# Attention, routing and expert layers in one kernel: row sums of shared blocks added with the even head, and another order of the attention plan

## The chip, the cores and the metric

One core of a Trainium2 chip runs the whole kernel in one launch. The metric is the device time of one execution in microseconds (us); the median of several runs counts. The engines are TensorE (PE, matmuls; PEld is its weight loads), VectorE (DVE), ScalarE (ACT), GpSimd (POOL) and SyncE (SP, which here only issues DMAs). Each executes its own queue in order.

## The reference

Attention over 2 x 8 heads of 576 rows and 64 columns with rotary embedding; a layer of eight experts of which each of 1152 tokens takes two; a dense feed-forward layer with softplus.

```python
scores = scale * np.matmul(q_rot, k_rot.transpose(0, 1, 3, 2))
scores = scores - np.max(scores, axis=-1, keepdims=True)
attn = np.exp(scores)
attn = attn / (np.sum(attn, axis=-1, keepdims=True) + 1e-09)
attn_out = np.matmul(attn, v)
...
top2 = np.argpartition(-noisy_logits, 2, axis=1)[:, :2]
h = np.maximum(x[mask] @ w1[e], 0.0)
out[mask] += top2_w[mask, k, None] * (h @ w2[e])
...
h = x @ w_in
g = np.maximum(h, 0.0) + np.log1p(np.exp(-np.abs(h)))
return g @ w_out
```

## The kernel before

Attention comes first, then the experts in order of their load, then the feed-forward layer. The last two are written out in their order; matmuls there are done in three parts (high by high, high by low, low by high half of a split number). The change touches attention alone, which is not written in an order: each step is entered in a table `plan` with engine, estimated cost, a due place and its predecessors (`op`, L1054), and `schedule` (L58) makes a list schedule of it: of the steps that can start, the one that starts earliest goes next, and of equal ones that with the smaller due place. `AHEAD` (L39) shifts the due place of each kind of step. The schedule's order is the order in which the instructions are written, and so that of each engine's queue.

Heads are worked in eight pairs p; head g is 2p or 2p + 1. A pair has nine blocks n of 128 score rows: four of each head, and a fifth, whose 128 rows are the last 64 of both heads. The steps, by their names in the plan:

- `S` (PE, `emit_S`, L486): scores of block n into one of two PSUM buffers, 4 matmuls, 8 for a shared block. `M` (DVE, L499): negated row maximum. `E` (ACT, `emit_exp`, L508): exponent, with the row sums as a second output (`acc`).
- `T` (PE, L517; the four columns that are left, L521 and L523), `Th` (ACT, L549), `Tl` (DVE, L553): transposes of the exponents for one block, their high and low halves. Two PSUM buffers `pt`.
- `A` (PE, L564, L566): two halves a = 0, 1 of the product with the values, 9 matmuls each, `Ao` (ACT) takes it out. `X` (PE, L586): transposes it back together with the gating logits. `rs` (POOL, `row_sum`), `ri` (DVE, L598): 1 / (row sum + 1e-9). `Xl`, `Xd` (DVE, L602, L611): scale logits and rows. `Xd` frees the PSUM buffer and, after an odd head, sends the rows to memory.
- `prep` (PE, L413), `ph`, `pl` (ACT, DVE): transposes of a pair's rotated queries and keys and their halves; `dq` and `dk` (SP, L449, L453): copy the queries, then the keys, to the other half of the partitions. The first `S` of pair p waits for `dk`. In pair 0 ACT does this instead (`k2`). `ro` and `rope` (POOL), for pair 0 `rf` (DVE): the rotation. `vs` (POOL): split of the values.
- `R`, `RP`, `RF`: routing of the first 512 tokens, in 14 steps; `cr`, `ga` (POOL, `gather_A`): gather the first expert's rows, which `XT` (PE, L1041), `XTh` and `XTl` transpose and split. `sp` (ACT, L183) and `sl` (DVE, the first two on POOL, L187): round and split six weight chunks.

PSUM buffers `pa` (two) are shared by `A`, `X`, `prep`, `XT` and the routing matmuls, in the order of their issue. In `row_sum` (L589) two small adds are done for each head: one for its four blocks, from `sums`, and one for its 64 rows of the shared block, from `sumL`.

Of the kernel before, what the change touches and what calls it, by code (L numbers as in the profile page):

```python
# [10 lines left out]
F32 = mybir.dt.float32  # L11
# [6 lines left out]
OP = mybir.AluOpType  # L18
# [4 lines left out]
B, H, S, D = 2, 8, 576, 64  # L23
N, DM, E, F1 = B * S, H * D, 8, 1024
# [13 lines left out]

AHEAD = {'A0': 30288.5, 'A1': 3627.5, 'Ao0': 4788.8, 'Ao1': -14676.7, 'E': 18585.3, 'L': -1902, 'M': 16742.7,  # L39
# [7 lines left out]
FC = 384  # L47
# [57 lines left out]
def fused_kernel(ctx: ExitStack, tc: tile.TileContext, q, k, v, w_gate, w_noise, noise, w1, w2,  # L105
                 w_in, w_out, cs_t, out):
    nc = tc.nc
# [205 lines left out]
    at1 = at_ctx.enter_context(tc.tile_pool(name="at1", bufs=1))  # L313
# [19 lines left out]
    sums = at1.tile([128, B, 5, H], F32, name="sums")  # L333
# [4 lines left out]
    PL = at1.tile([128, S], F32, name="PL")  # L338
    sumL = at1.tile([128, H], F32, name="sumL")

# [161 lines left out]
    def emit_exp(n):  # L502
        p, h, i = block(n)
        ps, nmx = stS.pop(n)
        g = 2 * p + h
        b = g // H
        acc = sumL[:, p:p + 1] if i == 4 else sums[:, b, i + b, g % H:g % H + 1]
        nc.scalar.activation(P_of(n).rearrange("p (a c) -> p a c", a=2), ps[:, :, :HN], AF.Exp, bias=nmx, scale=1.0,  # L508
                             accum_out=acc)
# [79 lines left out]
    def row_sum(g):  # L589
        b, h = divmod(g, H)  # L590
        nc.gpsimd.tensor_scalar(rinv[:, b, b:b + 4, h], sums[:, b, b:b + 4, h], 1e-9, None, op0=OP.add)
        q, j = slice(64 * b, 64 * b + 64), 4 - 4 * b
        x = 64 * (g % 2)
        nc.gpsimd.tensor_scalar(rinv[q, b, j:j + 1, h], sumL[x:x + 64, g // 2:g // 2 + 1], 1e-9, None, op0=OP.add)

# [467 lines left out]
    for n in range(NSTEP):  # L1063
        p, h, i = block(n)
        g, at_ = 2 * p + h, 10 * p + 5 * h + i
        twice = [("dk", p)] if p else [
            ("k2", x, u) for x in range(2) for u in ((0, 1, 2) if i == 4 else (h, 2))]
        need = twice + [("pl", p, u) for u in ((0, 1, 2) if i == 4 else (h, 2))]
        if i == 4:
            reads = [("T", g - 2, 5), ("T", g - 2, 4)] * (p > 0)  # L1070
        else:
            two = 2 * g + i // 2 - 3
            reads = readers(two // 2, two % 2 * 2 + i % 2) if two >= 0 else []
        op(("S", n), "PE", 1056 if i == 4 else 528, at_ - 4, need + [("S", n - 1)] * (n >= 1) + [("E", n - 2)] * (n >= 2), emit_S, n)
        op(("M", n), "DVE", 674, at_ + 7, [("S", n)], emit_max, n)
        op(("E", n), "ACT", 717, at_ + 69, [("M", n)] + reads +
           ([("rf", 5)] if n in (2, 3) else prep0 if n in (5, 6) else []), emit_exp, n)
    for g in range(2 * NP_):
        p, h = divmod(g, 2)
        for u in range(6 - h):  # L1080
            n = 5 * g + (0, 1, 2, 3, 3, 4)[u]
            blk = [9 * p + 5 * h + i for i in range(4)]
            src = [9 * p + 4] if u == 5 else blk[u:u + 1] if u < 4 else blk + [9 * p + 4] * (h == 0)
            op(("T", g, u), "PE", 400 if u != 4 else 200 if h else 300, n, [("E", e) for e in src], emit_T, g, u)
            old = (g - 2, g - 1) if u == 5 or u == 4 and h == 0 else (g - 2,)
# [9 lines left out]
        n = 5 * g + 5  # L1095
        op(("rs", g), "POOL", 620, n - 8000, [("E", 9 * p + i) for i in (range(4, 9) if h else range(5))], row_sum, g)
        op(("ri", g), "DVE", 190, n - 60, [("rs", g)], row_inv, g)
        op(("X", g), "PE", 1110, n - 24, [("Ao", g, 0), ("Ao", g, 1), ("c", 0)], emit_X, g)
        op(("Xl", g), "DVE", 150, n - 67, [("X", g), ("ri", g)], X_lg, g)
        op(("Xd", g), "DVE", 400, n - 67, [("Xl", g)], X_x, g)  # L1100
    for p in range(NP_):
        n = 10 * p
# [25 lines left out]
        if p:  # L1128
            op(("dq", p), "SP", 2000, n, [("pl", p, u) for u in range(3)] + [("S", 9 * p - 10)] * (p > 1), move_queries, p)
            op(("dk", p), "SP", 2000, n, [("dq", p)], keys_twice, p)  # L1130
    op(("in", 0), "SP", 5400, -300, [], lambda: None)
    op(("in", 1), "SP", 1300, -299, [("in", 0)], lambda: None)
# [21 lines left out]
    op(("cr", 0), "POOL", 2300, 100, [("R", 8)], choose_rest)  # L1154
    op(("ga", 0), "POOL", 2200, 100, [last[0], ("S", 62), ("vs", 7), ("Xd", 9)], gather_A)
    op(("gl", 0), "SP", 500, 100, [("ga", 0)], lambda: None)
# [519 lines left out]
```

## Time and profile before

| | |
|---|---|
| median of 3 runs | 661.6 us (661.05 to 663.89) |
| the profiled execution, its time and its span | 662.88 us, 661.1 us |
| busy in the span: PE, PEld | 622.8 us (94%), 560.9 us (85%) |
| busy: DVE, ACT, POOL | 482.0 (73%), 424.6 (64%), 218.0 us (33%) |
| mean granted clock of TensorE | 0.986 |
| DMA | 109.79 MB, mean 166 GB/s |

All rows below are from one execution. Attention takes the time up to about 188 us; there PE, DVE and ACT are all busy for most of the time. The experts and the feed-forward layer follow and are nearly all PE. A row of an engine in order of time gives the start, the duration, the line of the program, the instruction with what it writes and reads, and in brackets the idle time of that engine before it and what seems to have ended it. PEclk is the clock that was granted to TensorE as a share of its full speed: 1.0 is 2.4 GHz and 0.5 is 1.2 GHz.

### The profile page before, as it was taken

To read this page: it belongs to the slowest core of one execution; us is meant where nothing else is said; L and a number is where in the kernel's file an instruction comes from. 1 tells how busy PE (TensorE), PEld (TensorE's weight loads), DVE (VectorE), ACT (ScalarE), POOL (GpSimd) and SP (SyncE) were. 2 spreads that over 40 slices of the span, in tenths; PEclk is the share of its full clock that TensorE was granted. 3 is DMA by queue.
4 is the path that set the end of the run, shared out by engine and by line. 5 is a ranking of instruction groups with operands and counts; after the bars stand their busy time and mean duration, and the time that the engine had idled before them with its cause. 6 is when DMAs were issued, how large, how long until landed. Compare 5 with 4: busy or idle time off the path is not lost.

```text
span 661.1 us, 11470 instructions
## 1 busy us (share of the span) xinstructions
PE 622.8 (94%) x3922; PEld 560.9 (85%) x3922; DVE 482.0 (73%) x997; ACT 424.6 (64%) x887; POOL 218.0 (33%) x302
## 2 busy tenths in 40 slices
PE   3799999998798999999999999989999999999997
PEld 2699999898696998988889798968789999899996
DVE  6689888987774767859686776846996665676664
ACT  4788888877742666757667575736866544565553
POOL 6876766728545203341424231412310100000000
PEclk9899999999979999999999999998999999999999
DMA  6645465861635949998899989775410100100000
GB/s 156 152 100 136 124 149 126 267 185 39 203 113 183 321 150 315 334 332 291 315 311 323 312 291 351 273 222 176 144 49 32 34 17 0 49 1 1 33 0 33
DMA packets 69629, 109.79 MB, mean 166 GB/s; under 512 B 11616, under 2 KB 39008, under 8 KB 69120
## 3 DMA queue, kind: packets, MB, share of 16 engines
q1 hardware_dynamic: 63280, 93.31, 45.7%
q0 software_dynamic: 3136, 10.10, 4.6%
q10 hardware_dynamic: 3152, 5.62, 2.3%
q8 instruction: 32, 0.52, 0.3%
q14 instruction: 29, 0.24, 0.1%
HBM read 76.70 MB, written 23.59 MB: 152 GB/s over the span
## 4 chain that ended last, share of the span: by engine, by line
PE 62%; issue 3%; DVE 1%; DMA 1%; ACT 1%; POOL 0%; DVEq 0%; POOLq 0%; ACTq 0%
PE p L263 9%; PE p L264 9%; PE p L265 9%; PE ph L263 5%; PE ph L264 5%; PE ph L265 5%; PE po L265 5%; PE po L264 5%; PE po L263 5%; PE p L1242 2%; PE pa L1198 1%; PE p L1244 1%; DMA yg<-ytab,yrow 1%; PE px L1491 0%; DVE wc L187 0%
## 5 line engine op out<-in xcount | busy, mean ns | idle before, releaser
L187 DVE TENSOR_TENSOR w<-wraw,w 128x1024 fp32r<-128x1024 f32 x73 | 99.4, 1373 | 0.7 <-ACT w L183 0.7
L183 ACT ACTIVATE w<-wraw 128x1024 fp32r<-128x1024 f32 x75 | 78.8, 1056 | 12.9 <-DMA wraw<-in_moe_w_dram 12.1
L232 POOL TENSOR_TENSOR dm<-dm,da 128x512 int32<-128x512 int32 x32 | 42.0, 1312 | 134.1 <-DVE da L229 69.1
L264 PE MATMUL p<-xl,w 128*128 128x320 f32 (+3 forms) x256 | 77.5, 303 | 0.3 <-DVE xl L1201 0.3
L263 PE MATMUL p<-xh,w 128*128 128x320 f32 (+3 forms) x256 | 77.4, 302 | 0.0
L265 PE MATMUL p<-xh,w 128*128 128x320 f32 (+3 forms) x256 | 77.3, 302 | 0.0
L1554 ACT ACTIVATE fa<-ph 128x256 f32<-128x256 f32 (+1 forms) x64 | 26.0, 407 | 69.4 <-PE ph L265 69.4
L499 DVE TENSOR_REDUCE nmx<-ps 128x1 f32<-128x576 f32 x72 | 54.2, 753 | 17.6 <-PE ps L486 17.5
L263 PE MATMUL ph<-xh,w 128*128 128x256 f32 (+1 forms) x192 | 58.5, 305 | 1.0 <-ACT xh L1496 0.7
L263 PE MATMUL p<-w,hb 128*128 128x512 f32 x144 | 58.7, 407 | 0.0
L264 PE MATMUL ph<-xl,w 128*128 128x256 f32 (+1 forms) x192 | 57.5, 300 | 0.3 <-DVE xl L1497 0.3
L265 PE MATMUL ph<-xh,w 128*128 128x256 f32 (+1 forms) x192 | 57.4, 299 | 0.0
L1218 DVE SCALAR_TENSOR_TENSOR hb<-p,hb 128x256 fp32r<-128x256 f32 (+1 forms) x104 | 31.8, 347 | 34.1 <-ACT hb L1214 34.0
L265 PE MATMUL p<-w,hb 128*128 128x512 f32 x144 | 56.6, 393 | 0.0
L264 PE MATMUL p<-w,hb 128*128 128x512 f32 x144 | 56.5, 393 | 0.0
L549 ACT ACTIVATE pth<-pt 128x512 fp32r<-128x512 f32 x72 | 42.4, 599 | 18.3 <-PE pt L517 17.1
L1561 DVE TENSOR_SCALAR fu<-fa 128x256 f32<-128x256 f32 (+1 forms) x64 | 19.8, 309 | 47.0 <-ACT fa L1555 46.7
L553 DVE TENSOR_TENSOR ptl<-pt,pth 128x512 fp32r<-128x512 f32 x72 | 48.0, 684 | 5.8 <-ACT pth L549 5.4
L508 ACT ACTIVATE P<-ps,nmx 128x576 f32<-128x576 f32 x64 | 47.6, 744 | 4.5 <-DVE nmx L499 3.8
L1472 POOL DMA_INDIRECT yg<-ytab,yrow x18 | 19.0, 1055 | 91.2 <-PE px L1491 69.3
L264 PEld LDWEIGHTS p<-xl,w 128*128 128x128 f32 x256 | 48.2, 188 | 0.8 <-DVE xl L1201 0.5
L263 PEld LDWEIGHTS p<-xh,w 128*128 128x128 f32 x256 | 48.2, 188 | 0.6 <-ACT xh L1200 0.2
(321 smaller groups left out, 1830.5 us busy)
## 6 DMA issues: line engine op xcount, KB each, us to landing
wraw<-in_moe_w_dram SPq DMA_DIRECT2D x64, 512.0 KB
x<-in_moe_w_in_dram SPq DMA_DIRECT2D x16, 512.0 KB
x<-in_moe_w_out_dram SPq DMA_DIRECT2D x16, 512.0 KB
wtab<-dm SPq DMA_DIRECT2D x32, 256.0 KB
wraw<-wtab SPq DMA_DIRECT2D x16, 512.0 KB
ytab<-y ACTq DMA_DIRECT2D x18, 256.0 KB
kk<-kk SPq DMA_DIRECT2D x7, 640.0 KB
ytab<-zrow SPq DMA_DIRECT2D x4, 1024.0 KB
```

What stands on the lines that cost most here:

```text
L183: nc.scalar.activation(hi, r, AF.Copy)
L187: lo_eng.tensor_tensor(out=lo, in0=r, in1=hi.bitcast(F32), op=OP.subtract)
L232: nc.gpsimd.tensor_tensor(out=m, in0=m, in1=ai, op=OP.add)
L263: nc.tensor.matmul(ps, ah, bh, start=first and i == 0, stop=False)
L264: nc.tensor.matmul(ps, ah, bl, start=False, stop=False)
L265: nc.tensor.matmul(ps, al, bh, start=False, stop=last and i == n - 1)
L499: nc.vector.tensor_reduce(out=nmx, in_=stS[n][:, :, :HN], axis=AX.XY, op=OP.max, negate=True)
L508: nc.scalar.activation(P_of(n).rearrange("p (a c) -> p a c", a=2), ps[:, :, :HN], AF.Exp, bias=nmx, scale=1.0, accum_out=acc)
L549: nc.scalar.activation(dh, x, AF.Copy)
L553: nc.vector.tensor_tensor(out=dl, in0=x, in1=dh.bitcast(F32), op=OP.subtract)
L1218: nc.vector.scalar_tensor_tensor(out=o, in0=ps[:, c], scalar=0.0, in1=hh[:, c].bitcast(F32), op0=OP.max, op1=OP.subtract)
L1554: nc.scalar.activation(a, ps, AF.Abs)
```

## The change

Two things. `E` of a shared block writes its sums to `sums`, into the column of the even head, rather than to a tile of their own; `rs` of the even head adds the 1e-9 to the shared rows of both heads (two small adds), and `rs` of the odd head has none. `ga` gets `rs` of head 14 as a predecessor. And the plan has other costs for some steps and another table of shifts, which gives another order on all five engines.

```diff
-AHEAD = {'A0': 30288.5, 'A1': 3627.5, 'Ao0': 4788.8, 'Ao1': -14676.7, 'E': 18585.3, 'L': -1902, 'M': 16742.7,
...
+AHEAD = {'A0': 14597.4, 'A1': 35272.5, 'Ao0': -18382.3, 'Ao1': -17314.5, 'E': 8779.9, 'L': 6351.1, 'M': 29342.6,
...
-    sumL = at1.tile([128, H], F32, name="sumL")
...
-        acc = sumL[:, p:p + 1] if i == 4 else sums[:, b, i + b, g % H:g % H + 1]
+        acc = sums[:, b, 4 - 4 * b if i == 4 else i + b, g % H:g % H + 1]
...
-        q, j = slice(64 * b, 64 * b + 64), 4 - 4 * b
-        x = 64 * (g % 2)
-        nc.gpsimd.tensor_scalar(rinv[q, b, j:j + 1, h], sumL[x:x + 64, g // 2:g // 2 + 1], 1e-9, None, op0=OP.add)
+
+        r, j = slice(64 * b, 64 * b + 64), 4 - 4 * b
+        for x in range(2 - 2 * (g % 2)):
+            nc.gpsimd.tensor_scalar(rinv[r, b, j:j + 1, h + x], sums[64 * x:64 * x + 64, b, j:j + 1, h], 1e-9, None,
+                                    op0=OP.add)
...
-        op(("S", n), "PE", 1056 if i == 4 else 528, at_ - 4, need + [("S", n - 1)] * (n >= 1) + [("E", n - 2)] * (n >= 2), emit_S, n)
+        op(("S", n), "PE", 1100 if i == 4 else 540, at_ - 4, need + [("S", n - 1)] * (n >= 1) + [("E", n - 2)] * (n >= 2), emit_S, n)
...
-            op(("T", g, u), "PE", 400 if u != 4 else 200 if h else 300, n, [("E", e) for e in src], emit_T, g, u)
+            op(("T", g, u), "PE", 440 if u != 4 else 230 if h else 330, n, [("E", e) for e in src], emit_T, g, u)
...
-        op(("rs", g), "POOL", 620, n - 8000, [("E", 9 * p + i) for i in (range(4, 9) if h else range(5))], row_sum, g)
+        op(("rs", g), "POOL", 310 + 610 * (1 - h), n - 8000, [("E", 9 * p + i) for i in (range(4, 9) if h else range(5))], row_sum, g)
...
-        op(("X", g), "PE", 1110, n - 24, [("Ao", g, 0), ("Ao", g, 1), ("c", 0)], emit_X, g)
+        op(("X", g), "PE", 1130, n - 24, [("Ao", g, 0), ("Ao", g, 1), ("c", 0)], emit_X, g)
...
-            op(("dq", p), "SP", 2000, n, [("pl", p, u) for u in range(3)] + [("S", 9 * p - 10)] * (p > 1), move_queries, p)
-            op(("dk", p), "SP", 2000, n, [("dq", p)], keys_twice, p)
-    op(("in", 0), "SP", 5400, -300, [], lambda: None)
+            op(("dq", p), "SP", 2800, n, [("pl", p, u) for u in range(3)] + [("S", 9 * p - 10)] * (p > 1), move_queries, p)
+            op(("dk", p), "SP", 3500, n, [("dq", p)], keys_twice, p)
+    op(("in", 0), "SP", 7300, -300, [], lambda: None)
...
-    op(("ga", 0), "POOL", 2200, 100, [last[0], ("S", 62), ("vs", 7), ("Xd", 9)], gather_A)
+    op(("ga", 0), "POOL", 2200, 100, [last[0], ("S", 62), ("vs", 7), ("Xd", 9), ("rs", 14)], gather_A)
```

TensorE's queue before, ahead of the first `S` of pair 5 (the row with `qT`): `S`, the transposes T(8,5) of a shared block, `S`, X(7), T(8,3), then that `S`; T(9,0) and the first matmul of A(8,0) follow. (`PL` holds the exponents of a shared block, `P` the others, `yg` and `qT` the queries of even and odd pairs.)

```order
L486 MATMUL ps<-kk,yg 128x288 x4
L517 MATMUL pt<-ident,PL 128x128 x4
L486 MATMUL ps<-kk,yg 128x288 x4
L586 MATMUL pa<-Wx,o_149 128x96 x5
L517 MATMUL pt<-ident,P 128x128 x4
L486 MATMUL ps<-kk,qT 128x288 x4
L517 MATMUL pt<-ident,P 128x128 x4
L564 MATMUL pa<-pth,vhl_159 128x288
```

The same place now (the lines' numbers are one less here; the other matmuls of A(8,0) are left out):

```order
L585 MATMUL pa<-Wx,o_149 128x96 x5
L485 MATMUL ps<-kk,yg 128x288 x4
L516 MATMUL pt<-ident,P 128x128 x4
L485 MATMUL ps<-kk,yg 128x288 x4
L516 MATMUL pt<-ident,P 128x128 x4
L563 MATMUL pa<-pth,vhl_158 128x288
...
L563 MATMUL pa<-pt_157,vhl_158 128x288
L516 MATMUL pt<-ident,P 128x128 x4
L485 MATMUL ps<-kk,qT 128x288 x4
```

T(9,0), A(8,0) and T(9,1) have moved ahead of the pair's first `S`.

GpSimd's queue before, at the end of attention: the adds of head 14, the two gathers, a weight split, the adds of head 15, the second split, and the first sums of logits:

```order
L591 TENSOR_SCALAR rinv<-sums 128x4
L594 TENSOR_SCALAR rinv<-sumL 64x1
L1022 DMA w_2363<-xtab,idxA 128x512
L1022 DMA w_2363<-xtab,idxA 64x512
L187 TENSOR_TENSOR w_2369<-wraw,w_2369 128x1024
L591 TENSOR_SCALAR rinv<-sums 128x4
L594 TENSOR_SCALAR rinv<-sumL 64x1
L187 TENSOR_TENSOR w_2439<-wraw,w_2439 128x1024
```

The same place now:

```order
L590 TENSOR_SCALAR rinv<-sums 128x4
L594 TENSOR_SCALAR rinv<-sums 64x1 x2
L187 TENSOR_TENSOR w_2245<-wraw,w_2245 128x1024
L1023 DMA w_2361<-xtab,idxA 128x512
L1023 DMA w_2361<-xtab,idxA 64x512
L187 TENSOR_TENSOR w_2307<-wraw,w_2307 128x1024
L590 TENSOR_SCALAR rinv<-sums 128x4
```

The adds of the shared rows (64x1) both stand ahead of the gathers, one split is ahead of them too, and head 15's one add is behind both splits.

VectorE's queue before, from the last maximum on (`nmx`): T-halves (`ptl`) of head 15, reciprocals of heads 14 and 15, the halves of the left columns, logits and rows of head 14, the first gathered rows (`yg`) and the last T-half:

```order
L499 TENSOR_REDUCE nmx<-ps 128x1
L553 TENSOR_TENSOR ptl<-pt,pth 128x4x128
L598 RECIPROCAL rinv<-rinv 128x5
L553 TENSOR_TENSOR ptl<-pt,pth 128x4x128 x2
L598 RECIPROCAL rinv<-rinv 128x5
L553 TENSOR_TENSOR pt_158<-pt,pt_158 64x2x128 x2
L602 TENSOR_TENSOR lgt<-pa,rinv 128x5x16
L611 TENSOR_TENSOR xs<-pa,rinv 128x5x64
L465 TENSOR_TENSOR yg<-pa,yg 128x4x128
L553 TENSOR_TENSOR ptl<-pt,pth 128x4x128
```

The same place now:

```order
L498 TENSOR_REDUCE nmx<-ps 128x1
L552 TENSOR_TENSOR ptl<-pt,pth 128x4x128
L187 TENSOR_TENSOR w_2372<-wraw,w_2372 128x1024
L552 TENSOR_TENSOR ptl<-pt,pth 128x4x128 x2
L599 RECIPROCAL rinv<-rinv 128x5
L187 TENSOR_TENSOR w_2433<-wraw,w_2433 128x1024
L552 TENSOR_TENSOR pt_157<-pt,pt_157 64x2x128 x2
L552 TENSOR_TENSOR ptl<-pt,pth 128x4x128
L603 TENSOR_TENSOR lgt<-pa,rinv 128x5x16
L464 TENSOR_TENSOR yg<-pa,yg 128x4x128
L612 TENSOR_TENSOR xs<-pa,rinv 128x5x64
```

Two weight splits have come up among head 15's halves; the reciprocal of head 14 has gone ahead of the last maximum, and that of head 15 stands where it stood.

## Rows read from the trace of the kernel before

**Rows 1.** stages: us, busy of PE, PEld, DVE, ACT, POOL (instructions), PEclk, DMA share, GB/s
```profile
30.00:110.00 80.00, 75.64 (x601) 73.02 (x599) 70.41 (x134) 68.42 (x168) 55.25 (x86) 1.00 0.54 126
...
175.90:180.00 4.10, 0.55 (x6) 0.43 (x4) 2.17 (x6) 2.08 (x4) 2.42 (x2) 0.82 0.35 112
180.00:189.00 9.00, 8.44 (x38) 7.97 (x37) 6.66 (x10) 4.22 (x8) 3.79 (x6) 0.51 0.58 177
...
212.30:661.00 448.70, 440.66 (x2573) 389.76 (x2572) 315.75 (x634) 271.44 (x522) 81.23 (x69) 0.99 0.52 176
```

**Rows 2.** PE in order of time (start, us, what): first `S` of pairs 1, 4, 7
```profile
35.95 0.77 PE L486 MATMUL ps<-kk,qT 128*128 128x288 f32 x4 [0.73 <-ACT o L575]
...
91.84 0.77 PE L486 MATMUL ps<-kk,yg 128*128 128x288 f32 x4 [1.07 <-DMA kk<-kk]
...
153.04 0.76 PE L486 MATMUL ps<-kk,qT 128*128 128x288 f32 x4 [1.90 <-DMA kk<-kk]
```

**Rows 3.** SP in order of time: both copies of pair 4
```profile
82.04 1.77 SPq L449 DMA_DIRECT2D yg<-kk  x2
...
86.82 0.46 SPq L453 DMA_DIRECT2D kk<-kk  x1
```

**Rows 4.** PE in order of time: S(3)'s follower S(4)
```profile
24.88 2.29 PE L486 MATMUL ps<-kk,yg 128*128 128x288 f32 x8 [1.51 <-ACT P L508]
```

**Rows 5.** POOL in order of time: gathers and the small add
```profile
169.04 1.25 POOL L1022 DMA_INDIRECT w<-xtab,idxA  x1 [4.49 <-ACT pth L549]
170.59 0.92 POOL L1022 DMA_INDIRECT w<-xtab,idxA  x1 [0.30 <-issue]
...
177.50 0.23 POOL L594 TENSOR_SCALAR rinv<-sumL 64x1 f32<-64x1 f32 x1 [3.22 <-DMA w<-xtab,idxA]
```

**Rows 6.** DVE in order of time: reciprocal of head 15, rows of head 14
```profile
177.75 0.19 DVE L598 RECIPROCAL rinv<-rinv 128x5 f32<-128x5 f32 x1 [2.77 <-POOL rinv L594]
...
179.02 0.48 DVE L611 TENSOR_TENSOR xs<-pa,rinv 128x320 f32<-128x320 f32 x1
```

**Rows 7.** PE in order of time: S(71), second gathered rows, first expert matmul
```profile
167.89 0.78 PE L486 MATMUL ps<-kk,qT 128*128 128x288 f32 x4
...
179.60 0.66 PE L1041 MATMUL pa<-ident,w 64*128 64x64 f32 x4 [3.55 <-DVE xs L611]
...
187.67 0.51 PE L263 MATMUL p<-yg,w 128*128 128x192 f32 x1
```

**Rows 8.** PE in order of time: units
```profile
116.46 1.25 PE L586 MATMUL pa<-Wx,o 128*128 128x96 f32 x10
117.55 0.60 PE L517 MATMUL pt<-ident,P 128*128 128x128 f32 x4
117.91 0.78 PE L486 MATMUL ps<-kk,qT 128*128 128x288 f32 x4
118.52 0.28 PE L413 MATMUL pa<-ident,w 128*128 128x128 f32 x1
...
121.35 0.77 PE L486 MATMUL ps<-kk,qT 128*128 128x288 f32 x4
...
123.15 0.60 PE L517 MATMUL pt<-ident,P 128*128 128x128 f32 x4
```

**Rows 9.** DVE in order of time: last rope piece of pair 0
```profile
14.10 0.90 DVE L394 TENSOR_TENSOR P<-w,P 128x256 f32<-128x256 f32 x1
```

**Rows 10.** costliest groups (count, busy, mean ns, idle before): rounding of a weight chunk
```profile
L183 ACT ACTIVATE w<-wraw 128x1024 fp32r<-128x1024 f32 x75 | 78.8, 1056 | 12.9 <-DMA wraw<-in_moe_w_dram 12.1
```

**Rows 11.** DMA issues (count, us to landing), 168.9 to 170.3: first gather
```profile
w<-xtab,idxA POOLq DMA_INDIRECT x1, 5.1
```

**Rows 12.** POOL in order of time: equal adds
```profile
180.89 1.22 POOL L633 TENSOR_TENSOR lgt<-lgt 128x80 f32<-128x80 f32 x1
182.08 0.35 POOL L634 TENSOR_TENSOR lgt<-lgt 128x80 f32<-128x80 f32 x1
```

**Rows 13.** DVE in order of time: the weight split beside them
```profile
180.62 1.28 DVE L187 TENSOR_TENSOR w<-wraw,w 128x1024 fp32r<-128x1024 f32 x1
```

14 rows, old and new, of the table AHEAD are left out of this document.

## The prediction

> **What bounds the kernel now.** I read the table of stages first, then the waits of the matmul engine in order of time, then the instructions around each of them on the other queues. The stages [rows 1] say: in attention TensorE is busy 75.64 of 80 us (PE, 95%), VectorE 70.41 (88%), ScalarE 68.42; and after the hand-over to the expert layers PE is busy 440.66 of 448.7 us. So PE sets the time nearly everywhere, the expert part (untouched by the change) has 8 us of idle in all, and what the change can gain is PE's idle and slow time before about 212 us. It lies in three places.
>
> First, each head pair's first score block waits. Three of the seven such waits stand in [rows 2]: 0.73, 1.07 and 1.90 us (pairs 1, 4 and 7); the four others (pairs 2, 3, 5 and 6) lie between 0.73 and 1.90, and those of pairs 2, 3 and 5 between the first two. They stand before the first `S` of pairs 1 to 7. The view names the keys' copy for two of them and for others a ScalarE instruction that had long ended; in every pair the second copy (`dk`) was issued some 5 us earlier, so I put all of them down to it. For pair 4: first copy issued at 82.04, second at 86.82 [rows 3], block at 91.84 [rows 2]: 9.8 us from the split of the last keys to the first score.
>
> Second, the start: S(4) runs at 24.88 after a wait of 1.51 us [rows 4], since the keys of its second half are transposed, rounded and doubled after the first softmax blocks.
>
> Third, the end of attention. GpSimd issues the two gathers at 169.04 and 170.59; the small add behind them, for head 15's last rows, waits 3.22 us for the gathers' landing and runs at 177.50 [rows 5]. VectorE's reciprocal waits for it until 177.75, and behind that stand in its queue head 14's rows, which free a PSUM buffer at 179.02 + 0.48 [rows 6]; PE stands still 3.55 us until 179.60 [rows 7]. Then the granted clock of the stretch 180 to 189 is 0.51, against 1.00 before [rows 1]: this is the lower of TensorE's two levels, 1.2 GHz, after 4.1 us in which PE was busy 0.55 us.
>
> **Units.** From starts of neighbours in [rows 8]: `X` 1.09 us, four transposes `T` 0.36, a score block `S` 0.61 (its last block, for both heads, two of these); 123.15 - 121.35 holds one `S` and one `A`, so `A` is 1.2.
>
> **The change part by part.**
>
> *The code.* The 16 one-column adds stay 16: an even head now does two, an odd head none. GpSimd's work is the same to a few tenths. What goes is the one add that is queued behind the gathers and waits for them; head 15's remaining add reads `sums`, and the new dependence puts head 14's adds ahead of the gathers. Price on the path: in the next but one part.
>
> *Keys' copies.* In the new order PE has more to do between the last key transposes of a pair and that pair's first `S`. Counted in units, before against after: pair 1 6.6 against 8.4 us, pair 2 9.2 against 10.9, pair 3 9.2 against 10.4, pairs 4 and 5 9.2 against 11.4 and 10.8, pair 6 10.8 against 10.8, pair 7 10.6 against 10.9. For pairs 1 to 5 the extra 1.2 to 2.2 us are more than the waits (0.73 to 1.07), so these go: five times 0.73 to 1.07 is 3.7 to 5.4; I take 4.0. Pair 6 keeps its wait, pair 7 loses 0.4 of its 1.90. If VectorE's split comes late, the copies come late too and it is 1.5. The Trainium skill (DMA: Bandwidth & Descriptors, Anatomy of one DMA) fits a transfer as 2.0 us plus its bytes at 436 GB/s, an estimate of 6.8 us for the two copies of 576 and 640 KB, on the GpSimd path; by that the keys would be there in time and this term zero, but the 9.8 us of the trace decide. What is late next: the scores' own chain (below).
>
> *Start.* The transposes of pair 0's other half now stand ahead of S(0), so S(0) waits for VectorE's rope pieces (the addition that ends at 15.0 [rows 9] must now end before the transposes) and starts 2 to 3 us later than now; but keys and queries are then complete, and S(4) no longer waits for them. Between -1.5 and +2.5; I take +0.8.
>
> *End of attention.* From S(71) at 167.89 to the first expert matmul at 187.67 [rows 7] it is 19.8 us. PE's work there in units: `S` 0.6, six `T` 2.1, four `A` 4.8, two `X` 2.2, two transposes of gathered rows 0.7: 10.4. So 9.4 us are lost: 3.55 in the one wait, 3.5 by the slow clock (two `A` and one `X` at twice 1.2, 1.2 and 1.09), the rest in small waits. The set of work after S(71) is the same in the new order, but the reciprocal `ri` has no gather to wait for. What remains, read from the order: X(14) waits for ScalarE, which rounds a weight chunk (1.06 us [rows 10]) before it; A(15,0), A(15,1) and X(15) each wait for a PSUM buffer or for `Ao`; together I reckon 3.4. The first gathered rows are now transposed before T(15,4); the first gather landed 5.1 us after its issue [rows 11], and PE has about as much to do, so 0 to 1.8 there, I take 0.5. Slow clock: the idle time now lies in pieces of about 1 us instead of one of 3.55; between 0 (clock kept) and 3.5 (as now); I take 1.2, since the 1.90 us of pair 7 left the clock alone. There is one more price: VectorE's weight split now stands ahead of head 15's transposes while GpSimd does a split too. The trace shows these two engines getting in each other's way: GpSimd's add of 80 elements takes 0.35 us alone and 1.22 [rows 12] while VectorE's split runs from 180.62 [rows 13]. I take 0.8 of 0 to 2.3. The Trainium skill (SBUF — State Buffer, SBUF: two separate sides) says that whichever of the two begins first holds the port for its whole instruction; by that VectorE could lose the rest of a GpSimd split, 1.2 instead of the 0.8. Sum of what remains: 3.4 + 0.5 + 1.2 + 0.8 = 5.9, so the gain is 9.4 - 5.9 = 3.5, between 0 and 8. The routing chain, gathers and loads behind all start from X(15), so they move with it; weights for the first expert are split by then.
>
> *New waits.* Three weight chunks are rounded on ScalarE before the last exponent instead of one, and the scores run less far ahead: PE's work between a score block and its transposes falls from 7.4 to 5.2 us in the mean (units, over the 64 blocks that are transposed alone). The trace of before has no such wait to price; bounds are nothing and PE's whole present idle time in the steady part (80 - 75.64 = 4.4 us per four pairs, so about 9). I take 1.9, nearer to nothing, because VectorE and ScalarE both keep over 10% idle.
>
> *Sum.* 4.0 + 0.4 + 0.8 + 3.5 - 1.9 = 6.8. The profiled execution took 662.88 us; minus 6.8 is 656.1. It lies 1.3 above the median of the runs, 661.6, so the median should come to 654.8: I say 655.0.
>
> **The rivals.**
> *A: the key waits only change their name.* The scores' chain (score, maximum, exponent, transpose) becomes what PE waits for, and the freed 4.0 us come back. For: VectorE at 88% has little room, and the lead is shorter. Against: the counts leave 5.2 us of PE work over a chain of about 2.5. Then 655 + 4 to 5: 659 to 660.
> *B: the end stays late.* Head 15's add stands behind both gathers and now behind both GpSimd splits; if the reciprocal still waits there, or the first gather holds PE at its transposes, the 3.5 us are not gained: 658.5. Against: the add's 3.22 us were a wait for the landing, and no instruction of that queue waits for it in the new order.
> *C: slower.* VectorE becomes the bound in the steady part: every block's scores wait for a maximum that is queued behind splits. It decides when a pair loses more than 0.85 us (6.8 over eight pairs); at 1.5 us per pair the time is 661.6 - 6.8 + 12 = 667. Against: VectorE's own busy time per pair does not grow.
> *D: the waits of [rows 2] are not the copies'*, as the fit of the page would have it; then the 4.4 us of that term are not there: 659.
>
> **How the numbers follow.** 0.5%, about what a measurement of this kernel tells from no change, is 3.3 us: faster means under 658.3, slower over 664.9. Forecast (gain of 4 to 12): 0.66. A 0.14, within 0.5%. B 0.08, half of it under 658.3. C 0.09, slower. D 0.03, within. So faster 0.70, same 0.21, slower 0.09. The range for 8 in 10 goes from the sum with the better ends of start and last stretch (clock kept, no port loss: about 649.5) to beyond A, B and D, 661.5; outside are C and a little on the lower side.
>
> **What would show it.** Right: no wait of PE over 0.3 us before the first `S` of pairs 1 to 5; pairs 6 and 7 still wait 1 to 1.5; no wait for a gather on GpSimd; nothing over 2 us on PE between S(71) and the first expert matmul, and that stretch about 16 us; the expert part within 1 us of 448.7. Wrong: many waits of PE for ScalarE's exponent in the middle (A, C), the clock at its lower level before 170 us, or a first gather that PE stands still for (B).

## The result, and the profile after

The kernel after takes 654.06 us (median of 4 executions, 651.58 to 655.72), the kernel before beside it 662.75 (4, 661.05 to 664.55). The ratio is 0.9858, with a 95% interval of 0.9832 to 0.9884. 655.0 was predicted, in a range of 649.5 to 661.5.

The profiled execution of after took 655.72 us with a span of 653.9 (before: 661.1). Four stretches between landmarks show where the 7.2 us went: the start up to S(4), the scores from S(4) to S(71), the end of attention from S(71) to the first expert matmul, and the rest. The rows are those of the stages (us, busy time of PE, PEld, DVE, ACT and POOL with their instructions, granted clock, DMA share, GB/s); first before, cut at the landmarks:

```profile
0.00:24.88 24.88, 10.70 (x43) 8.37 (x43) 16.34 (x33) 12.94 (x26) 18.37 (x23) 1.00 0.61 155
24.88:167.89 143.01, 133.59 (x1057) 129.27 (x1058) 122.45 (x244) 118.12 (x291) 94.73 (x168) 0.99 0.56 144
167.89:187.67 19.78, 15.22 (x94) 13.92 (x92) 13.58 (x24) 13.51 (x26) 10.99 (x11) 0.77 0.69 211
187.67:661.10 473.43, 463.26 (x2735) 409.34 (x2734) 329.60 (x697) 280.02 (x545) 93.93 (x101) 0.99 0.51 172
```

The same of after, and two rows that answer to the first and the last of [rows 1]:

```profile
0.00:23.51 23.51, 9.62 (x43) 8.90 (x43) 15.89 (x32) 12.51 (x25) 16.70 (x22) 1.00 0.61 157
23.51:162.39 138.88, 134.51 (x1060) 128.12 (x1058) 124.20 (x250) 118.89 (x295) 99.00 (x171) 1.00 0.62 159
162.39:180.51 18.12, 15.21 (x92) 13.31 (x91) 14.87 (x20) 11.59 (x25) 7.76 (x10) 0.81 0.52 155
180.51:653.90 473.39, 462.66 (x2735) 408.77 (x2734) 329.06 (x697) 279.90 (x545) 93.43 (x101) 1.00 0.51 172
...
30.00:110.00 80.00, 77.86 (x613) 74.66 (x614) 70.42 (x134) 67.14 (x167) 56.34 (x62) 1.00 0.57 134
205.00:653.90 448.90, 440.38 (x2571) 389.60 (x2571) 314.73 (x634) 271.07 (x522) 80.76 (x69) 1.00 0.52 175
```

The start gains 1.37 us, the scores 4.13, the end of attention 1.66, the rest 0.04. In the scores PE's idle time fell from 9.42 to 4.37 us; in the 80 us of [rows 1] PE is now busy 77.86 instead of 75.64.

**Key waits.** The seven waits before the first `S` of a pair were 7.37 us in before (0.73, 0.87, 0.77, 1.07, 0.76, 1.27 and 1.90; three stand in [rows 2]). Of them one is left, in pair 3, by PE's rows in order of time:

```profile
71.91 0.77 PE L485 MATMUL ps<-kk,qT 128*128 128x288 f32 x4 [0.33 <-DMA kk<-kk]
...
128.28 0.73 PE L485 MATMUL ps<-kk,yg 128*128 128x288 f32 x4
...
147.18 0.79 PE L485 MATMUL ps<-kk,qT 128*128 128x288 f32 x4
```

The last two are the first blocks of pairs 6 and 7, without a wait. SP issued their copies, the queries' and the keys', at

```profile
117.70 1.60 SPq L448 DMA_DIRECT2D yg<-kk  x2
123.24 0.46 SPq L452 DMA_DIRECT2D kk<-kk  x1
...
136.73 1.64 SPq L448 DMA_DIRECT2D qT<-kk  x2
141.43 0.46 SPq L452 DMA_DIRECT2D kk<-kk  x1
```

**End of attention.** PE from the last score blocks on (the first row holds S(70) and S(71), which I put at 161.78 + 0.61 = 162.39):

```profile
161.78 1.51 PE L485 MATMUL ps<-kk,qT 128*128 128x288 f32 x8
...
169.24 0.63 PE L1042 MATMUL pa<-ident,w 128*128 128x128 f32 x4 [1.87 <-DMA w<-xtab,idxA]
...
171.44 2.45 PE L585 MATMUL pa<-Wx,o 128*128 128x96 f32 x10 [0.43 <-ACT o L574]
...
180.51 0.34 PE L263 MATMUL p<-yg,w 128*128 128x192 f32 x1
```

GpSimd and VectorE there (after's answer to [rows 5, 6]):

```profile
164.26 0.91 POOL L1023 DMA_INDIRECT w<-xtab,idxA  x1 [0.30 <-issue]
165.20 2.39 POOL L187 TENSOR_TENSOR w<-wraw,w 128x1024 fp32r<-128x1024 f32 x1
165.37 3.31 DVE L187 TENSOR_TENSOR w<-wraw,w 128x1024 fp32r<-128x1024 f32 x1
167.68 1.10 POOL L590 TENSOR_SCALAR rinv<-sums 128x4 f32<-128x4 f32 x1
```

No add waits for a gather any more. But PE waits 1.87 us for the landing of the first gather, and VectorE's split, 1.28 us in [rows 13], takes 3.31: it starts 0.17 us after GpSimd's split and ends 1.09 us after it (168.68 against 167.59), as if it had run behind it. GpSimd's add of 128x4 (L590), 0.23 to 0.24 us in the runs below, takes 1.10 beside VectorE's split. And the clock falls once more, here in one window of the stages (from 169 to 170 us and from 177 us on it is 1.00):

```profile
170.00:176.00 6.00, 5.49 (x24) 4.69 (x24) 4.38 (x8) 3.74 (x8) 0.92 (x3) 0.50 0.70 230
```

For 6 us PE works at 1.2 GHz (0.50): `X`, 1.25 us in [rows 8], takes 2.45.

### The profile page after: what moved, and what is told of

Same layout as the page of the kernel before. It is cut to its first block, busy times and chain, and to the rows that moved or that the text cites. A ratio compares the mean times of both kernels' runs of the same rounds, so it can differ in the third digit from the quotient of the medians.

```text
span 653.9 us, 11488 instructions
## 1 busy us (share of the span) xinstructions
PE 622.0 (95%) x3922; PEld 559.1 (85%) x3922; DVE 484.0 (74%) x997; ACT 422.9 (65%) x887; POOL 216.9 (33%) x302
## 4 chain that ended last, share of the span: by engine, by line
PE 61%; issue 3%; DVE 2%; ACT 1%; DMA 1%; POOL 1%; DVEq 0%; POOLq 0%; ACTq 0%
PE p L263 9%; PE p L264 9%; PE p L265 9%; PE ph L263 5%; PE po L265 5%; PE po L264 5%; PE ph L265 5%; PE po L263 5%; PE ph L264 5%; PE p L1243 2%; PE pa L1199 1%; PE p L1245 1%; DMA yg<-ytab,yrow 1%; PE px L1492 0%; DVE wc L187 0%
```

## Experiments

Ratios are against executions of before taken beside them on the same chip, whose median was 662.75, 663.51, 665.57 or 665.12 us.

### The two parts of the change apart

The new sums in the old order:

```diff
-        acc = sumL[:, p:p + 1] if i == 4 else sums[:, b, i + b, g % H:g % H + 1]
+        acc = sums[:, b, 4 - 4 * b if i == 4 else i + b, g % H:g % H + 1]
...
-        nc.gpsimd.tensor_scalar(rinv[q, b, j:j + 1, h], sumL[x:x + 64, g // 2:g // 2 + 1], 1e-9, None, op0=OP.add)
+        for x in range(2 - 2 * (g % 2)):
+            nc.gpsimd.tensor_scalar(rinv[r, b, j:j + 1, h + x], sums[64 * x:64 * x + 64, b, j:j + 1, h], 1e-9, None,
+                                    op0=OP.add)
```

> The order of before with the new row sums alone: head 15 has no add behind the gathers. Theory (that add set the 3.55 us stall of TensorE, and the stall set the low clock): VectorE's 2.77 us wait at the reciprocal is gone; the second gathered rows still cannot be transposed before they land, about 6.9 us after 170.6, so 1 to 1.5 us of the stall stay. From S(71) to the first expert matmul 17.5 us (clock low later) to 14.5 (clock kept) instead of 19.8; whole time 1.5 to 5 us under the kernel before. The part up to S(71) at 167.9 as before. Rival (the gathers' landing or the rest of the chain sets the end, the gain is all in the order): stretch over 19 us, time within 1 us of before.

Measured: 661.6 us (10 executions), ratio 0.9979 (0.9952 to 1.0005): no gain that can be told from none. GpSimd's and PE's rows in order of time:

```profile
171.40 0.92 POOL L1023 DMA_INDIRECT w<-xtab,idxA  x1 [0.30 <-issue]
...
174.84 0.24 POOL L590 TENSOR_SCALAR rinv<-sums 128x4 f32<-128x4 f32 x1
...
178.58 0.43 PE L1042 MATMUL pa<-ident,w 64*128 64x64 f32 x4 [2.32 <-DMA w<-xtab,idxA]
```

The add now runs at 174.84 without a wait, as intended. But PE's wait at the second gathered rows only falls from 3.55 [rows 7] to 2.32 us and has another name: these rows, issued at 171.40, come 7.2 us later. The small add had hidden that wait, for the same gather. In this execution the end of attention takes 17.92 us (168.10 to 186.02) instead of 19.78.

The new order with the old sums (the table, the costs and the predecessor of `ga` as in after; `sumL` and the old `row_sum` back in):

> The new order with the old row sums: head 15's second add stands behind the gathers again and waits for their landing. Theory (order and sums are two separate gains, the order the larger): S(71) at 162.4 as in the changed kernel; the add waits till about 171 (second gather issued at 164.3, 6.7 us later), the reciprocal of head 15 1.0 to 1.5 us later than 169.8, the stretch from S(71) to the first expert matmul 19 to 20 us instead of 18.1; time 1 to 2 us over the changed kernel, 5 to 7 under the kernel before. Rival (the sums carry the gain): time within 3 us of before.

Measured: 654.26 us (651.76 to 656.46), ratio 0.9874 (0.9821 to 0.9927), the same as after. The add that had held up the end waits for the gathers here too, but little:

```profile
166.73 0.63 PE L1041 MATMUL pa<-ident,w 128*128 128x128 f32 x4 [0.73 <-DMA w<-xtab,idxA]
...
168.60 0.23 POOL L594 TENSOR_SCALAR rinv<-sumL 64x1 f32<-64x1 f32 x1 [1.11 <-DMA w<-xtab,idxA]
```

The end of attention was expected at 19 to 20 us and took 16.8 (160.43 + 0.61 to 177.88), with the clock at 1.00; that is 0.7 us more than after takes at the same clock (16.06, below). So the whole measurable gain is the order's; in it the new sums are worth nothing that shows in the time.

### Are the waits the keys' copies?

The kernel before, in which the second copy moves only the high halves of the keys (the low halves are not copied):

```diff
-        nc.sync.dma_start(out=t[64:128], in_=t[0:64])
+        nc.sync.dma_start(out=t[64:128, 0], in_=t[0:64, 0])
```

> The kernel before, with the second copy of each pair cut to half its bytes: only the high halves of the keys are copied, the low halves in the other 64 partitions are left out. Theory (the seven waits before each pair's first score block, 7.4 us together, are for the keys' copy): the copy lands 1 to 1.5 us sooner, five waits of 0.7 to 1.1 vanish or fall under 0.3, those of pairs 6 and 7 fall below 0.7, S(71) starts at 162 to 164 instead of 167.9. Rival (the waits are the softmax chain's, the copies landed before): the waits stay 0.7 to 1.9, S(71) at 167.4 to 168.4.

And the kernel after with the copies of the queries issued twice:

```diff
-        for x in range(2):
+        for x in (0, 1, 0, 1):
```

> The changed kernel, with both query copies of each pair issued twice (the same bytes to the same place), so that the keys' copy starts later. Theory (the new order has hidden the copies with a margin under 1 us): the keys' copy is issued 1 to 2.5 us later, waits of 0.5 to 2 us come back before the first score block of pairs 1 to 7, S(71) at 166 to 174 instead of 162.4. Rival (the waits were something else's): no wait over 0.4 us there, S(71) within 1 us of 162.4.

Measured, half the keys: 652.15 us in one execution. None of the seven first blocks waits any more, and from S(4) to S(71) it takes 133.01 us instead of 143.01:

```profile
25.05:158.06 133.01, 130.77 (x1057) 127.59 (x1058) 121.80 (x244) 117.62 (x291) 94.84 (x168) 1.00 0.51 132
```

The copy did not only become smaller: it also depends on the first copy of the queries alone, and so is issued 3.2 to 3.3 us after the first of them in five of the seven pairs (4.1 in pair 4, 6.7 in pair 6), where in before it is 4.5 to 5.2 (6.7 in pair 6).

Measured, queries twice: 686.02 us in one execution. The list of PE's waits has all seven again (us in total, number, the longest), and SP's and PE's rows of one pair show why:

```profile
PE ps L485 <- DMA kk<-kk: 20.9, 7, 3.8
```

```profile
47.86 5.07 SPq L448 DMA_DIRECT2D yg<-kk  x4
55.62 0.46 SPq L452 DMA_DIRECT2D kk<-kk  x1
```

```profile
61.10 1.22 PE L485 MATMUL ps<-kk,yg 128*128 128x288 f32 x7 [2.17 <-DMA kk<-kk]
```

The keys' copy is issued 7.8 us after the queries', and PE's block starts 5.5 us after that. The waits are 20.9 of the 32 us that this version loses against after; the clock also falls behind five of them. Both runs went further than expected, in the expected direction: whether a pair's first block waits hangs on these two copies, one behind the other.

### A cure of the key waits without a new order

Before, nothing left out; the second copy is issued as four, the first head's parts first:

```diff
-        nc.sync.dma_start(out=t[64:128], in_=t[0:64])
+        for h in range(2):
+            for x in range(2):
+                nc.sync.dma_start(out=t[64:128, x, h], in_=t[0:64, x, h])
```

> The kernel before, its order unchanged and nothing left out: the second copy of a pair (dk, 640 KB) is issued as four copies of 160 KB, the first head's high and low halves ahead of the second head's, so that the pair's first score blocks need 320 KB of it. Theory (the seven waits before the first score blocks, 7.37 us together, are the copies'): they fall to under 2.5 us in sum, the last score block comes 4 to 7 us before 167.89, and with an end of attention as in before the time falls by 4 to 7: 657 to 660. Rival (what counts is only when dk can be issued, not its size, or four issues cost as much as they save): the waits stay over 5 us in sum and the time within 2 us of before.

Measured: 654.19 us (651.78 to 656.58), ratio 0.9858 (0.9818 to 0.9898). SP's rows of pair 4, which answer to [rows 3], and the stages from S(4) to S(71) and on to the first expert matmul:

```profile
77.64 1.77 SPq L449 DMA_DIRECT2D yg<-kk  x2
...
81.30 2.76 SPq L455 DMA_DIRECT2D kk<-kk  x4
```

```profile
24.95:157.91 132.96, 130.74 (x1058) 127.54 (x1058) 121.82 (x244) 117.47 (x291) 94.79 (x168) 1.00 0.59 150
157.91:177.38 19.47, 15.07 (x93) 13.47 (x92) 13.70 (x24) 13.72 (x26) 10.99 (x11) 0.82 0.81 249
```

All seven waits are gone and the scores take 132.96 us, 10.05 less than before and 5.9 less than in after; the end of attention stays as in before (19.47). So the key waits alone are worth as much as the whole change. PE's idle time there fell by 7.2 (9.42 to 2.22) and its busy time by 2.85. About 1.7 of the latter is the clock, 1.00 in this stretch; in before it falls at S(4), by two stage rows of before:

```profile
25.00:25.50 0.50, 0.50 (x2) 0.50 (x3) 0.15 (x1) 0.50 (x2) 0.50 (x2) 0.50 0.67 47
25.00:30.00 5.00, 4.75 (x24) 4.42 (x24) 2.67 (x4) 2.98 (x8) 2.90 (x6) 0.67 0.85 180
```

A mean of 0.67 over 5 us is 3.3 us at the lower level, at half the speed. These 1.7 us are not the split's: the clock is down from 25.0 us on, the first copy of pair 1 is issued only at 26.07, and up to there both kernels run the same order. So about 8.3 of the 10.05 us can be the split's, still more than the 7.37 us of the waits. The other 1.2 us of busy time are not settled.

### The start alone

The kernel before, with the first 59 steps of the order taken from after (all up to S(4)):

```diff
+    first = [...]
+    names = first + [n for n in names if n not in first]
```

> The kernel before, with the first 59 steps of the order (everything up to the score block S(4)) taken from the kernel after, and the rest as before. Theory (the start gains 1.4 us and the gain is carried on, since TensorE is the bound behind it): S(0) at about 15.3 after a wait of about 5 us for VectorE's rope pieces, S(4) at about 23.5 (24.88 in before), the last score block also 1 to 1.5 us earlier than the 167.89 of before, the seven key waits as before, the time about 660 to 662 in this one look. Rival (the early start is lost at the first key wait, since that is set by VectorE and the copies): the last score block within 0.3 us of 167.89.

Measured: 664.25 us in one execution (before beside it: 665.12). S(4) starts at 23.40, 1.5 us earlier, but then, by SP's and PE's rows:

```profile
30.97 0.46 SPq L453 DMA_DIRECT2D kk<-kk  x1
```

```profile
36.27 1.12 PE L486 MATMUL ps<-kk,qT 128*128 128x288 f32 x4 [3.73 <-DMA kk<-kk]
```

Pair 1's first block starts at 36.27, later than the 35.95 of [rows 2]: its keys are no earlier, and the gain turns into a wait of 3.73 us. The last score block starts at 168.46, 0.57 us later than in before. My theory fell; the rival's cause held, though its 0.3 us were passed too. In after that block starts at 34.19, since the keys' copy is issued there at 29.09 instead of 30.71: the start counts only with pair 1's copies.

### The end of attention: port, landing, clock

Three versions of after with steps moved in the order. In the first, head 15's add stands ahead of the second of GpSimd's two weight splits (not of both, as its expectation has it: the first split stays ahead of the gathers); in the second the transposes of the first gathered rows stand behind those of head 15's third block; the third has both:

```diff
+    names = moved(names, ('rs', 15), ('E', 71))
+    names = moved(names, ('sl', 1), ('rs', 15))
+    names = moved(names, ('sl', 2), ('sl', 1))
...
+    names = moved(names, ('XT', 0), ('T', 15, 2))
```

> The kernel after, with GpSimd's two last operations of attention in another place: head 15's add stands ahead of the two weight splits of GpSimd, not behind them. In the kernel after, VectorE's split (3.31 us, from 165.37) began while GpSimd's split ran, and GpSimd's add (1.10 us) began while VectorE's ran. Theory (the port that the two engines share is held by whichever starts first): VectorE's split takes about 1.2 us, GpSimd's add 0.2 to 0.4, so head 15's parts come 2 us earlier; but the transposes of the first gathered rows still wait for the landing, about 1.9 us, so the stretch from the last score block to the first expert matmul (18.12 us in after) gives up at most 0.5: about 653.5 us, no difference that can be measured. Rival (the port is what holds the end): the stretch shrinks by 2 us, about 652.

> The kernel after, with the transposes of the first gathered rows moved on TensorE behind the transposes of head 15's third block. Theory (two waits stand side by side, the rows' landing and VectorE's split that is held up by GpSimd's): the 1.9 us wait at the gathered rows falls under 0.5, but the next wait, for the low parts of head 15's first block behind the held split, grows by 1 to 1.9; the stretch of 18.12 us keeps within 0.5: about 653.5 us. Rival (the landing alone holds the end): the stretch shrinks by 1.9 us, and if the clock stays at its upper level by 4 to 5: 649 to 652.

> Both moves at once: GpSimd's add ahead of the splits and the gathered rows' transposes later. Theory (both waits have to go): no wait of TensorE over 1.1 us between the last score block and the first expert matmul, the granted clock stays at its upper level for most of it, and the stretch goes from 18.12 to between 14 and 16.5 us: 650 to 652. If something else holds the end (ScalarE's weight rounding, or the PSUM buffers of the outputs), the stretch stays over 17 and the time within 1 us of the kernel after.

In the fourth, PE has something to do while it waits:

```diff
+        if name == ('XT', 0):
+            ps = psS.tile([128, 2, 512], F32, name="ps")
+            for j in range(14):
+                nc.tensor.matmul(ps[:, j % 2, :HN], QT[7][:, 0:128], KK[7][:, 0, 0, 0:HN], start=True, stop=True)
```

> The kernel after, with 14 matmuls of no use (into a free PSUM buffer, read by nothing) put on TensorE in front of the transposes of the first gathered rows, where it waits 1.87 us for the landing. Theory (the lower clock, 0.50 from about 170 to 176.6 us in after, follows from this idle time and costs about 3 us): the clock stays at 1.00 through the stretch, which goes from 18.12 to about 15.5 us although work is added: about 651.5. Rival (the clock is incidental to the end, which is held by other engines): the clock stays up but the stretch stays at 17.5 to 18.5 us.

And the kernel after and the first version again, beside each other:

> The kernel after once more, on the same chip as the next, for a comparison of the two. 651.5 to 656, median near 654; by the theory of the clock (its lower level after the wait for the gathered rows costs about 3 us) the executions with a mean clock of 1.000 lie near 652 and those with 0.992 near 655.5.

> The version with GpSimd's last add ahead of its two weight splits, once more. If the freed port is worth 2 us at the end and keeps the clock up more often, the median lies 1.5 to 3 us under that of the kernel after in the same call; if the earlier look was chance, within 1 us of it.

The kernel after had its clock at 1.00 through this stretch in its second profiled execution, so that the two show its price. Its stage row and its wait at the gathered rows:

```profile
162.30:178.36 16.06, 12.75 (x92) 10.80 (x91) 14.85 (x20) 11.60 (x25) 7.91 (x10) 1.00 0.53 173
```

```profile
168.54 0.63 PE L1042 MATMUL pa<-ident,w 128*128 128x128 f32 x4 [1.30 <-DMA w<-xtab,idxA]
```

The same instructions take 16.06 us instead of 18.12: 2.06 less, of which 0.57 is the shorter wait (1.30 for 1.87). Which it is differs from one execution to the next. Of the ten executions of after, the three with a mean clock of 1.000 took 651.58, 651.93 and 652.82 us, and the two with 0.992 and 0.993 took 655.72 and 655.30. But the end of attention is not the only place: this second profiled execution, with the clock kept there, took 654.96 us all the same. Far behind attention its PE waits longer at one place (2.42 us, 1.62 in the first execution), and the clock is then at 0.50 for about 7 us instead of 3 to 4:

```profile
433.75 0.66 PE L1492 MATMUL pa<-ident,yg 128*128 128x128 f32 x4 [2.42 <-DVE yg L1486]
```

```profile
435.00:440.00 5.00, 3.43 (x12) 2.21 (x11) 2.04 (x3) 1.24 (x3) 0.00 (x0) 0.50 0.74 210
```

So a mean clock, or a time, does not tell what the end of attention did; only the stage row does.

*Add first.* 651.74 us (ratio 0.9816, 0.9768 to 0.9865); the second time 652.01 (0.9834, 0.9795 to 0.9874) beside 653.6 of after (0.9833, 0.9803 to 0.9863). The rows of VectorE's split, GpSimd's add, VectorE's next split and PE's gathered rows, and the stage:

```profile
164.94 1.22 DVE L187 TENSOR_TENSOR w<-wraw,w 128x1024 fp32r<-128x1024 f32 x1
...
166.39 0.23 POOL L590 TENSOR_SCALAR rinv<-sums 128x4 f32<-128x4 f32 x1 [1.45 <-ACT P L507]
...
167.76 2.39 DVE L187 TENSOR_TENSOR w<-wraw,w 128x1024 fp32r<-128x1024 f32 x1
...
168.01 0.63 PE L1042 MATMUL pa<-ident,w 128*128 128x128 f32 x4 [1.09 <-DMA w<-xtab,idxA]
```

```profile
162.00:177.34 15.34, 12.28 (x93) 10.83 (x91) 13.92 (x20) 11.57 (x25) 7.99 (x10) 1.00 0.63 182
```

This split and the add are as short as alone, so what lengthened them was that they ran beside the other engine's work. But the clash has moved, it has not gone: GpSimd's split now runs from 166.70 to 169.07, and VectorE's next split, which took 1.18 us in after, takes 2.39 and ends 1.08 us behind it. On the path the move is worth 0.7 us at the same clock (15.34 against 16.06; 15.40 the second time), not the 2.1 that VectorE's first split lost: behind it PE waits for the landing anyway. The medians differ by 1.6 us, which the second expectation counted as an effect (1.5 to 3), but the ratios are the same and the six executions spread from 651.28 to 657.80, so it can't be told from after.

*Rows later.* 654.24 us, as after; the stretch takes 17.0 us (160.98 + 0.61 to 178.62), shorter than the expected 17.6 to 18.6, with a mean clock of 0.90. The wait for the landing is gone, and in its place PE waits for VectorE behind the held split:

```profile
164.56 3.59 DVE L187 TENSOR_TENSOR w<-wraw,w 128x1024 fp32r<-128x1024 f32 x1
164.66 2.40 POOL L187 TENSOR_TENSOR w<-wraw,w 128x1024 fp32r<-128x1024 f32 x1
...
168.81 0.69 PE L520 MATMUL pt<-ident,P 128*128 128x128 f32 x2 [2.24 <-DVE ptl L552]
```

*Both.* 653.13 us, 1.1 us over the expected 650 to 652; no wait over 1.1 us, but waits of 0.90 and 0.84 come later, and the clock falls there (0.50 from 174 to 176):

```profile
162.60:179.26 16.66, 14.06 (x92) 12.11 (x91) 14.00 (x20) 11.62 (x26) 7.87 (x10) 0.90 0.59 168
```

*Filled.* 658.21 us instead of the expected 651.5. After was not run beside it; the three versions above were, and each of the four executions (657.74 to 658.50) is slower than all of theirs (to 654.97). The stretch is about what was expected, 16.0 us (162.20 + 0.61 to 178.83) with the clock at 1.00. But later, in the expert part, PE stands still in the middle of one tile's transposes, in an idle time that the profile gives no cause for, and then the clock falls:

```profile
201.38 0.58 PE L1209 MATMUL pa<-ident,xg 128*128 128x128 f32 x2 [2.81 <-issue]
```

```profile
200.00:207.00 7.00, 5.62 (x16) 3.73 (x16) 0.69 (x1) 0.60 (x1) 1.68 (x4) 0.51 1.04 338
```

From the first expert matmul to the end it takes 477.3 us instead of 473.39. An idle time of 1.8 us ahead of these transposes stands in every version, the 2.81 us only in this one; why 14 more matmuls bring them stays open.

## Why the prediction was right, and where its terms were off

The sum was 6.8 us and the profiled execution gained 7.2. The places of the gain were right, and so was its cause at the keys' copies; at the end of attention the cause was right only in part. That the sum came so close is in part luck, since the misses of the terms cancel:

- **Keys' copies, 4.4 predicted; 7.04 of waits went.** The two copies set these waits, as [rows 2, 3] were read: with half of the keys copied they go, with more copies they grow to 20.9 us. Rival D, which went by the fit of the Trainium skill (DMA: Bandwidth & Descriptors, Anatomy of one DMA), is out by the three experiments on the copies; that fit, for the GpSimd path, gives an estimate of 6.8 us for the two transfers, where the blocks of pairs 1, 4, 6 and 7 still waited for them 9.8 to 12.1 us after the first issue. The mis-sized part is pairs 6 and 7. I had left them 1.27 and 1.5 us, since PE's work ahead of their first `S` did not grow. They have no wait at all, because their copies were faster: from the first copy's issue to the block it is 10.6 and 10.5 us without a wait, against 12.1 and 11.9 with one before. For pair 6 SP's queue shows other traffic in another place: a copy of zeros is issued directly behind the keys' copy in before (127.62, behind 127.11) and 4.4 us behind it in after (127.68, behind 123.24). For pair 7 it shows no such thing, and that this made the copies faster is not shown.
- **New waits, -1.9 predicted; -2.9.** PE's idle time other than the seven waits grew by 2.0 us (9.42 - 7.37 = 2.05 before, 4.37 - 0.33 = 4.04 after), as priced, and its busy time by 0.9. In the latter 1.1 us are work that stands behind S(4) now (PE is busy 9.62 us ahead of it, 10.70 before), and 1.7 were given back by the clock, which did not fall at S(4) and which I had not in the sum (with before's order it fell there in two of four profiled executions, so this part can be chance); so another 1.5 us of longer busy time have no explanation. The split copies show the cost: with the old order they gain 10 us in this stretch, where the new order gains 4.1, each with these 1.7 in it. Rival A's price was thus partly paid, rival C's was not.
- **Start, 0.8 predicted; 1.37**, inside its bounds. But as an edit of its own it was worth nothing in the one execution of it: the step that was missing in the working is that S(4)'s time counts only if pair 1's keys come earlier too.
- **End of attention, 3.5 predicted; 1.66 in the profiled execution, 3.7 in the second one** (19.78 - 16.06). The reason given was the lesser part of it: taking the add away from behind the gathers left a wait of 2.32 us for the gather itself. The landing was put at 0.5 us and is 1.30 to 1.87. The slow clock was put at 1.2, between 0 and 3.5; it is either nothing or about 1.5 to 2.1, by the execution. One half of rival B came true here: the first gather does hold PE at its transposes, 1.87 us, which I had named as a sign of being wrong. The port was put at 0.8; taking the first clash away is worth 0.7 on the path. VectorE itself loses 2.1 us there (3.31 for a split that takes 1.22 alone), more than the 1.2 that I had worked out. The Trainium skill (SBUF — State Buffer, SBUF: two separate sides) has the first of the two engines hold the port for its whole instruction; the trace agrees with it where GpSimd's split is the first (by 0.17 us here). In the version with the rows later and in the second execution of after VectorE's split is the first by its recorded start, by 0.10 and 0.02 us, and still ends 1.09 us behind GpSimd's; so either GpSimd's recorded starts are off by that much, or the rule does not give the order; which it is, no run here shows.
- **The expert part**, within 1 us of 448.7: 448.90.

Of what was to show it: no wait over 0.3 us in pairs 1 to 5 (but for one of 0.33), no wait for a gather on GpSimd and nothing over 2 us on PE at the end (1.87) came true; the 1 to 1.5 us in pairs 6 and 7 and the 16 us at the end (18.12, though 16.06 at the upper clock) did not. The median, 654.06, hides a miss each way: too little for the keys, too much for the end.

A version with the split copies and the new order's end was not run, and none of the runs is faster than after beyond its interval.

## What to carry to other kernels

When an instruction waits for a transfer through a helper, look at who else needs the same transfer: taking the helper away moves the wait to the next reader. Before giving an order more slack for a copy, try a smaller first piece of the copy, the part that the first reader needs; here three lines did what a new order of the whole plan did. A gain at the start counts only as far as the next transfer's issue moves with it. And before you put a difference between two profiles down to an edit, look whether it begins ahead of everything that the edit moved, as the clock's fall at S(4) did.

## What the runs showed of the hardware

- The granted clock of the same stretch of the same kernel differs from one execution to the next: 1.00 throughout, or 0.50 for 6 us, behind a wait of PE of 1.30 and of 1.87 us. From 25 to 30 us it was at 0.67 and 0.66 in the profiled executions of before and of the new sums alone, at 1.00 with the keys halved or split, in the same order up to there, and in the new order; with the start alone it fell after the wait of 3.73 us instead (0.66 from 35 to 40 us). The length of the wait ahead does not settle it: with the queries copied twice the clock fell behind a key wait of 2.17 us and not behind those of 2.41 and 2.96 us. The ten executions of after spread over 4.1 us; the two profiled ones differ in the clock at two places, at the end of attention and from about 435 us on.
- Two splits of the same size on VectorE and GpSimd that start within 0.2 us of each other run one behind the other, VectorE's second each time: 3.31 us instead of 1.22 where it starts 0.17 us later, 3.59 and 3.51 where it starts 0.10 and 0.02 us earlier; each ends 1.09 us behind GpSimd's. A GpSimd add of 128x4 beside VectorE's split goes from 0.23 to 1.10 us.
- The keys' copy of 640 KB split in four takes SP 2.70 to 5.50 us to issue instead of 0.46, and the first reader still starts earlier.
